# First two block sums of W2 in one group of matmuls, a new order of all steps, and 103 matmuls of constants

## The chip, the cores and the metric

The kernel runs on one core of a Trainium2 chip. Its time is the device time of one execution in microseconds, taken as the median of several runs. The engines of the core are TensorE (PE, matrix products into PSUM), VectorE (DVE), ScalarE (ACT), GpSimd (POOL) and SyncE (SP, which here only issues DMAs). Each engine works through its own queue in order; semaphores hold an instruction until what it needs is there.

## The reference

The reference is a two-way attention between tokens and a small state, followed by a feed-forward block:

```python
def _attn_ref(x, state):                      # x (8, 8, 512, 64), state (8, 8, 32, 64)
    scores = scale * np.matmul(x, state.transpose(0, 1, 3, 2))
    a = softmax(scores)
    xread = np.matmul(a, state)
    scores2 = scale * np.matmul(state, x.transpose(0, 1, 3, 2))
    a2 = softmax(scores2)
    sread = np.matmul(a2, x)
    return np.concatenate([xread, sread], axis=2)

def _moe_ref(x, g_ln, w_ch1, w_ch2):          # x (8, 544, 512), W1 (512, 2048), W2 (2048, 512)
    xn = (x - mu) / np.sqrt(var + 1e-06) * g_ln
    return x + np.maximum(xn @ w_ch1, 0.0) @ w_ch2
```

Here `softmax` stands for subtracting the row maximum, the exponential and dividing by the sum plus 1e-9, and mu and var are the mean and the variance of a row. The heads are joined between the two parts, so that a row of the second part has 512 values.

## The kernel before

All products are made in float16, with each operand split into a high and a low half and three of the four partial products kept. The feed-forward width of 2048 is cut into four *units* of 512. The work falls into these pieces, each a Python generator that yields one step after another:

- `weights1(u)`: loads one unit of W1 in two halves, packs the words, takes column means by matmuls (`means`, line 600), subtracts them, sums absolute values by matmuls with a constant matrix `ones` (`add`, line 609), scales, and splits into halves that DMAs carry to `w1c`.
- `weights2(u)`: the same kind of work for one unit of W2, which ends in `w2h[u]`.
- `attention(b)`: the attention of batch b; `state_products(b)`: the state times W1, which gives `matrix[b][u]` (line 666).
- `first_products` and `second_products_by_unit`: the feed-forward block of batch 0, unit by unit as the weights arrive (lines 702 and 716).
- `sums_of_weights(u)`: for batches 1 to 7 the second product is made by a scheme of Strassen's kind, with seven block products in place of eight. It needs sums of blocks of W2. For each unit u and each half n, four sums are made in turn: t3 = B22 - B12, then B12 - B11 (written over B12), then t2 = B22 minus the new B12, then n4 = B21 - t2. Each is four matmuls with plus or minus the identity (`signs`, line 748) into half a PSUM bank; ACT copies it out as the high half and DVE writes the low half. The first and second sum share a bank, and the third and fourth share another.
- `products(b)`: for each of two groups of columns and each unit a hidden block (`first`, line 794; for the state rows `first_of_state`, line 803) and the block products (`multiply`, line 850), then `together`, which adds the pieces up and stores.

PSUM has three pools: `ps_f` with four banks (`acc`), `ps_a` with one pair (`banks`) and `ps_d` with two banks (`half`). A tile is given a bank when a step first uses it.

The order of all steps is written out by hand in the constant `PLAN`. An entry `19:3-5` means: issue items 3 to 5 of stream 19. Streams are numbered in the order of the list `streams`: 0 the gain, 1 attention of batch 0, 2 to 5 `weights1`, 6 `state_products(0)`, 7 `first_products`, 8 to 11 `weights2`, 12 the common scale, 13 to 16 `second_products_by_unit`, 17 and 18 attention and state products of batch 1, 19 to 22 `sums_of_weights`. From 23 on each batch has eighteen streams of products (a hidden block and its block products for each of eight units and groups, in turn, with `together` at the end of each group of four) and then the attention and the state products of the next batch; so 37 and 39 are block products of batch 1, 38 the hidden block of 39, and 42 the state products of batch 2. `issue` walks the plan and issues each item, so the plan sets the order on every engine's queue. In `sums_of_weights` items 0, 3, 6 and 9 are the matmuls of the four sums for n = 0, each with its ACT copy and its DVE step behind it, and 12, 15, 18 and 21 those for n = 1. The plan need not keep items of one stream together: between 19:0 and 19:3 it may put other streams' items, and 19:1 on either side of 19:3.

The page names every step that goes through the helper `do` by line 187, and matmuls by their own lines.

Of the kernel before, what the change touches and what calls it, by code (L numbers as in the profile page):

```python
# [201 lines left out]
def moe_attention(ctx: ExitStack, tc: tile.TileContext, x, state, g_ln, w1, w2, out):  # L202
# [539 lines left out]
    def sums_of_weights(u):  # L742
# [8 lines left out]
        for n in range(2):  # L751
# [5 lines left out]
            for k, (d, a, b) in enumerate(((t3, b22, b12), (b12, b12, b11), (t2, b22, b12), (n4, b21, t2))):  # L757
                yield do(subtract, k % 2 == 0, o[k], *a, *b)
                yield do(nc.scalar.activation, d[0], o[k], AF.Copy)
                yield do(nc.vector.tensor_tensor, d[1], o[k], d[0], ALU.subtract)  # L760
# [206 lines left out]
```

## Time and profile before

| | us |
|---|---|
| median of 3 runs | 695.02 |
| lowest and highest run | 693.15, 695.36 |
| the profiled execution | 693.68 |
| its span, from first to last instruction | 691.9 |
| mean granted clock of PE | 0.977 of full |

The page gives busy times of each engine over the span; a window table gives the same for stretches of time, with the clock that PE was granted. The waits list, for each engine and line, what ended its idle time. A timeline row has the start, the time taken, the engine, the line, the operation with what it writes and reads, how many of its kind are merged in the row, and in brackets the idle time just before it with its releaser. All these rows come from the one profiled execution.

### The profile page before, as it was taken

What the parts mean: (1) busy time and instruction counts of PE and PEld (TensorE: products, weight loads), DVE (VectorE), ACT (ScalarE), POOL (GpSimd) and SP (SyncE); (2) the same over time, 40 slices, a digit from 0 to 9 for tenths busy, and PEclk for the clock granted to TensorE, in tenths of its full rate; (3) what the DMA queues carried; (4) which work ended last, traced back from release to release, by engine and by line L of the source; (5) the groups of instructions that cost most, each with busy time, mean ns of one, the idle gap of its engine ahead of it and who ended that gap; (6) DMA issues with size and microseconds to landing.
All of it is one profiled execution on the core that took longest, in us unless ns stands there. A gap on an engine that the chain in (4) does not pass through costs nothing.

```text
span 691.9 us, 14637 instructions
## 1 busy us (share of the span) xinstructions
PE 633.4 (92%) x5945; PEld 494.0 (71%) x5948; DVE 498.7 (72%) x1002; ACT 387.9 (56%) x699; POOL 215.9 (31%) x189
## 2 busy tenths in 40 slices
PE   0648897989998999999999998999999999999996
PEld 0224554546986798778877987688868877889885
DVE  4999886467666676878787777776787687646733
ACT  5498797465654565556555654475456554435332
POOL 0002242330422332533423342433444233423322
PEclk9979898999999999999999999999999999999999
DMA  8898868125340344134213330453223503144221
GB/s 326 273 253 227 245 170 163 24 39 127 95 67 17 81 124 72 38 91 139 58 47 77 95 56 20 101 135 68 64 65 110 105 1 74 39 108 77 63 63 30
DMA packets 98563, 69.63 MB, mean 101 GB/s; under 512 B 72704, under 2 KB 90624, under 8 KB 98048
## 3 DMA queue, kind: packets, MB, share of 16 engines
q1 hardware_dynamic: 96384, 64.77, 36.9%
q0 software_dynamic: 864, 3.15, 2.4%
q8 instruction: 46, 0.75, 0.5%
q10 hardware_dynamic: 1248, 0.79, 0.4%
q14 instruction: 21, 0.17, 0.1%
HBM read 28.05 MB, written 9.44 MB: 54 GB/s over the span
## 4 chain that ended last, share of the span: by engine, by line
PE 74%; DVE 14%; ACT 7%; DMA 2%; issue 2%; POOL 0%; ACTq 0%; DVEq 0%
PE acc L850 34%; PE half L794 18%; PE acc L716 5%; PE half L666 4%; PE half L803 3%; DVE rs L187 2%; PE acc L748 2%; PE acc L702 2%; PE acc L600 2%; ACT xs L187 2%; DVE w_t L187 2%; ACT sums L187 1%; DVE ts L187 1%; ACT eB L187 1%; DMA w1c<-sums 1%
## 5 line engine op out<-in xcount | busy, mean ns | idle before, releaser
L850 PEld LDWEIGHTS <-xs 128*128 128x128 f16 x2520 | 243.2, 98 | 43.3 <-issue 14.0
L187 POOL TENSOR_TENSOR xs<-rs,xs 128x512 f16<-128x512 f32 x120 | 140.3, 1181 | 270.6 <-ACT xs L187 206.9
L850 PE MATMUL acc<-w2h,xs 128*128 128x256 f16 x1440 | 184.1, 274 | 0.0
L794 PE MATMUL half<-ea,matrix 128*128 128x256 f16 x1344 | 162.7, 273 | 6.1 <-DVE matrix L187 2.7
L794 PEld LDWEIGHTS <-matrix 128*128 128x128 f16 x1344 | 130.2, 98 | 26.0 <-issue 8.0
L850 PE MATMUL acc<-sums,xs 128*128 128x256 f16 x1080 | 141.6, 273 | 0.0
L187 DVE SCALAR_TENSOR_TENSOR rs<-half,rs 128x256 f32<-128x256 f32 x224 | 89.9, 419 | 34.4 <-ACT xs L187 14.7
L187 ACT ACTIVATE xs<-half 128x256 f16<-128x256 f32 (+1 forms) x112 | 54.0, 487 | 89.3 <-DVE rs L187 39.0
L187 ACT ACTIVATE xs<-rs 128x512 f16<-128x512 f32 (+1 forms) x128 | 77.6, 619 | 41.3 <-DVE rs L187 37.5
L187 DVE SCALAR_TENSOR_TENSOR xs<-half,xs 128x256 f16<-128x256 f32 (+1 forms) x112 | 61.1, 550 | 32.4 <-ACT xs L187 30.5
L187 ACT ACTIVATE matrix<-half,hs 128x512 f16<-128x512 f32 x56 | 37.7, 684 | 30.4 <-PE half L666 30.2
L187 DVE SCALAR_TENSOR_TENSOR matrix<-half,hs,matrix 128x512 f16<-128x512 f32 x56 | 41.0, 742 | 15.3 <-ACT matrix L187 15.3
L716 PE MATMUL acc<-w2h,hid 128*128 128x512 f16 x192 | 43.1, 379 | 0.0
L187 DVE TENSOR_TENSOR strip<-acc,strip 128x256 f32<-128x256 f32 (+1 forms) x60 | 33.3, 555 | 11.8 <-PE acc L850 8.0
L187 ACT ACTIVATE rs<-half 128x256 f32<-128x256 f32 x56 | 21.3, 380 | 31.2 <-PE half L794 19.4
L666 PE MATMUL half<-w1c,sT 128*32 128x512 f16 x448 | 33.8, 384 | 2.5 <-DVE xs L187 1.2
L716 PEld LDWEIGHTS <-hid 128*128 128x128 f16 x192 | 18.5, 98 | 22.3 <-issue 1.9
L600 PE MATMUL acc<-w_t,gm 128*128 128x512 f32 x32 | 18.2, 725 | 15.7 <-DVE w_t L187 15.7
L187 POOL TENSOR_TENSOR hid<-strip,hid 128x512 f16<-128x512 f32 x16 | 19.8, 1244 | 39.5 <-ACT hid L187 39.4
L187 POOL TENSOR_TENSOR ts<-ts,mA 128x1024 f32<-128x1024 f32 (+1 forms) x8 | 15.4, 1919 | 51.5 <-DVE of_weights L187 30.1
L702 PE MATMUL acc<-ea,matrix 128*128 128x256 f16 x192 | 26.9, 301 | 2.1 <-ACT strip L187 1.1
L187 POOL TENSOR_TENSOR ts<-ts,dA 128x1024 f32<-128x1024 f32 (+1 forms) x8 | 14.4, 1806 | 45.3 <-DVE of_weights L187 23.6
(152 smaller groups left out, 783.0 us busy)
## 6 DMA issues: line engine op xcount, KB each, us to landing
raw<-in_moe_w_ch_dram SPq DMA_DIRECT2D x9, 1024.0 KB, 10.4
out_dram<-xr SPq DMA_DIRECT2D x16, 512.0 KB, 3.2
x_f<-in_x_dram SPq DMA_DIRECT2D x15, 512.0 KB, 5.6
sums<-in_moe_w_ch_dram SPq DMA_DIRECT2D x7, 1024.0 KB, 6.1
ek<-ea SPq DMA_DIRECT2D x56, 64.0 KB, 2.1
ek<-ek SPq DMA_DIRECT2D x7, 512.0 KB, 4.3
xr<-part POOLq DMA_DIRECT2D x6, 512.0 KB, 5.0
w1c<-raw SPq DMA_DIRECT2D x8, 256.0 KB, 4.2
```

The lines of the kernel that those rows point to most:

```text
L187: return lambda: f(*map(now, args), **{k: now(v) for k, v in kw.items()})
L600: nc.tensor.matmul(ps, lhsT=gm[:, k:k + 1].broadcast_to([P, P]), rhs=t4[:, k], start=k == 0, stop=k == 3)
L666: nc.tensor.matmul(ps[32 * j:32 * j + 32], lhsT=sT[:, g, a, 32 * j:32 * j + 32], rhs=w[:, 2 * g + j // 2, j % 2], start=a == 0, stop=a == ...
L702: nc.tensor.matmul(o[:, 256 * f:256 * f + 256], lhsT=m[:, g, i, P * (q + f):P * (q + f) + P], rhs=ea[:, s, k, g], start=f == 0 and g == 0 ...
L716: nc.tensor.matmul(po, lhsT=hid[:, i, q, c * P:(c + 1) * P], rhs=w[:, j, q], start=first and q == 0 and n == 0, stop=last and q == 3 and n ...
L748: nc.tensor.matmul(o, lhsT=signs[:, k // 2], rhs=v[k], start=start and k == 0, stop=k == 3, skip_group_check=True)
L794: nc.tensor.matmul(ps[:, 256 * q:256 * q + 256], lhsT=m[:, h, i, P * (2 * k + q):P * (2 * k + q) + P], rhs=ea[:, 0, j, h, 256 * g:256 * g ...
L803: nc.tensor.matmul(ps[:, 256 * q:256 * q + 256].rearrange("p (t n) -> p t n", t=2), lhsT=w[:, k // 2, k % 2, fs] if k < H else wn[:, k - H ...
L850: nc.tensor.matmul(po[o], lhsT=y[:, n, i, o] if o < 2 else x[:, o - 2, n, i], rhs=v[j], start=u == 0 and n == 0 and k == 0 and o in (2, 1, ...
```

## The change

It has three parts.

In `sums_of_weights` the matmuls of the first two sums (t3 and the new B12) become one item of eight matmuls, followed by the ACT and DVE steps of both. The third and the fourth sum stay items of four. The same matmuls run with the same operands into the same half banks. A stream of sums has 22 items now: for n = 0 the matmuls are items 0, 5 and 8, for n = 1 items 11, 16 and 19.

A new stream, 175, has 103 items. Each is one matmul of the constant `ones` (bf16, 128 x 128) with itself repeated four times (512 columns) into one tile of the pool `half` that nothing reads. They all stand in the early part of the plan: nine ahead of the first transposition of batch 0's maxima, then in groups of up to 23 between the steps of W1, the last block of eight ahead of 1:90, and three single ones behind it.

The plan is written anew for the whole kernel, with the turns that tiles take on PSUM banks accounted for. Unit 2 of W1 is treated first, then units 1, 0 and 3; before, it was 1, 0, 2 and 3. Most lines of both plans are left out here.

```diff
 PLAN = (
...
-    "7:0 1:66-67 7:1-2 7:4-5 9:0 6:9-10 9:2 7:3 7:6-7 5:12 5:9 7:12-13 5:11 7:8 5:13 17:12 17:2 17:11 5:14 6:11 8:3 "
...
-    "19:15 17:25 14:9-10 14:1 17:26-27 17:19 19:16 10:16-17 11:2 11:4 7:49 14:3 10:18-19 11:5 14:4 14:2 7:32 19:0 "
-    "7:33-34 19:17 11:6-7 19:13-14 11:8 19:1 7:35 19:3-5 20:0-1 20:3 7:44 20:2 7:45-46 17:28 17:36 17:33 15:1 17:5 "
-    "11:9 17:37 18:9 7:42 14:5 7:50 19:2 7:47 7:51 11:10-13 11:15 12:0 17:39 20:12 12:1-2 20:13-14 20:4 18:12 "
-    "20:15-16 20:5 20:17 17:4 18:10 15:3 17:3 17:6 17:34-35 15:2 7:43 17:38 17:49 15:4-5 18:11 7:52-53 7:56-58 11:14 "
...
-    "18:15 17:54 18:3 21:12 22:15 22:13 7:61 18:16 22:14 18:4 18:17 41:2 19:18 21:13-14 7:62 17:40 21:15-16 18:5 "
...
-    "18:1-2 22:17 21:6-8 18:18 22:0-1 22:3 20:21 22:2 18:19-20 20:22-23 41:3 22:4-5 23:0 23:2 23:4 23:1 23:3 21:18 "
...
+    "1:0 1:3-4 1:1-2 1:5 175:0-8 1:6-7 175:9 1:8-12 4:1 1:19 1:72 0:0 4:6 1:20 1:24-25 4:5 4:7 4:0 4:3 1:17-18 4:2 "
+    "4:4 3:1 3:6 1:22-23 1:13-14 3:5 3:7 3:0 3:3 175:10-32 4:8 3:2 1:15 3:4 175:33-36 3:8 2:0 2:3 4:9 4:12 1:21 4:11 "
+    "4:10 2:2 2:4 4:13 1:16 1:27-29 3:10 3:9 3:11 1:44 175:37-39 4:14-15 1:45-46 1:26 175:40 1:30 3:12-13 1:31 1:33 "
+    "1:47 1:34 1:48 1:35 2:1 2:6 175:41-54 3:14 2:5 4:16 5:0 5:3 17:1 5:1 2:7 3:15 1:49 3:16 1:37 1:36 1:38-39 "
+    "175:55-60 2:8 9:0 17:0 1:50 3:17 5:2 5:5 1:62 1:40 3:18-19 8:0 3:22 2:11 4:17 2:12 1:63 2:9-10 2:13 1:64 "
+    "175:61-73 1:73 1:79 1:75 1:32 2:14 3:21 1:76 5:4 4:18-19 4:21 1:80 1:51 2:15 1:58 5:6 2:16-19 2:22 17:10 5:7 "
+    "1:77-78 9:2 2:21 3:20 3:24 3:23 2:20 175:74-79 5:8 5:12 1:59-60 17:7 2:23-24 17:8 175:80-90 6:9 8:2 1:52-53 6:6 "
+    "1:74 5:11 5:10 5:9 5:13-14 6:10 1:54-55 4:20 1:56-57 6:11 5:15 6:3 6:7 1:65 17:9 6:4 5:16-18 175:91 6:0-1 6:5 "
+    "1:66-67 8:1 175:92-99 1:90 1:94 5:19 8:5 1:95 6:2 7:0 1:91-92 7:1 7:4 8:6 1:93 7:2 8:3-4 8:7 1:41 8:8 4:23 7:5 "
...
+    "5:21 175:100 8:11 7:7 8:12-13 17:14 8:15 8:14 7:13 175:101-102 17:15-18 6:13-14 1:71 7:14 1:88 1:81 8:18 6:17 "
...
+    "6:21-23 9:4-5 9:7 7:27 6:19 1:83 6:20 7:28 7:36-37 13:8 10:1 7:18 1:84-85 1:98-99 7:38 10:6 9:8 7:19 7:29 1:96 "
...
+    "10:7 10:4 10:8 13:10 10:9-10 7:50 7:35 7:31 7:41 17:29 11:2 19:11 10:11 7:51 10:12-16 10:18 10:17 10:19 17:30 "
...
+    "11:18-19 12:1 17:28 15:3 20:0 20:3 20:14 12:2 20:12-13 41:2 17:33 15:4-5 18:4-5 17:19 20:4 15:8-9 41:11 20:1-2 "
+    "20:15 15:6-7 15:10 21:11 21:14-15 17:36-37 17:39 17:38 17:40 18:7-8 21:12 7:56-58 17:4 20:16 21:16 7:59 17:3 "
...
+    "17:41-43 17:46 20:21 17:44-45 17:60-61 17:66 16:3-4 16:1-2 17:62 16:6 22:14 16:7 17:65 22:0-1 22:3 17:70 "
...
+    "22:5-6 21:5-7 17:77 25:9 27:5 25:10 17:78 22:7 21:8-9 17:79 21:10 17:80 17:85-87 25:13 22:19-21 17:88 25:11-12 "
...
+    "38:5-6 41:61 41:66 38:4 38:10 38:8 36:12 37:2 61:5 16:5 61:11 38:7 17:73 38:9 42:6-7 41:62 39:0 38:13-14 "
...
+WARM = 103
...
-            for k, (d, a, b) in enumerate(((t3, b22, b12), (b12, b12, b11), (t2, b22, b12), (n4, b21, t2))):
-                yield do(subtract, k % 2 == 0, o[k], *a, *b)
-                yield do(nc.scalar.activation, d[0], o[k], AF.Copy)
-                yield do(nc.vector.tensor_tensor, d[1], o[k], d[0], ALU.subtract)
+            for pairs in (((t3, b22, b12), (b12, b12, b11)), ((t2, b22, b12),), ((n4, b21, t2),)):
+                first = len(o)
+                def subtract_all(*v, first=first):
+                    for k in range(len(v) // 5):
+                        subtract(first != 1 and k == 0, *v[5 * k:5 * k + 5])
+                todo = [(d, a, b, o.pop(0)) for d, a, b in pairs]
+                yield do(subtract_all, *[v for d, a, b, p in todo for v in (p, *a, *b)])
+                for d, a, b, p in todo:
+                    yield do(nc.scalar.activation, d[0], p, AF.Copy)
+                    yield do(nc.vector.tensor_tensor, d[1], p, d[0], ALU.subtract)
...
+    warm = half()
+
+    def warmth():
+        for _ in range(WARM):
+            yield do(nc.tensor.matmul, warm, lhsT=ones, rhs=ones.unsqueeze(1).broadcast_to([P, 4, P]), start=True, stop=True)
+
+    streams.append(list(warmth()))
     issue(tc, streams, PLAN)
```

220 rows, old and new, of the table PLAN are left out of this document.

## The prediction

> **What bounds the kernel now.** I read the page first (busy times), then the busy table by stage, then the waits of TensorE (PE), then the timeline at the waits.
>
> ```profile
> span 691.9 us, 14637 instructions
> PE 633.4 (92%) x5945; PEld 494.0 (71%) x5948; DVE 498.7 (72%) x1002; ACT 387.9 (56%) x699; POOL 215.9 (31%) x189
> ```
>
> PE is the bound over the whole: 92% busy. What a new order can win is PE's idle time, 691.9 - 633.4 = 58.5 us, and the stretches in which its clock is below full. By stage (columns: busy us of PE, weight load, DVE, ACT, POOL, then granted clock, DMA share, GB/s):
>
> ```profile
> 20.00:80.00 60.00, 42.28 (x339) 22.84 (x341) 56.56 (x98) 46.23 (x61) 8.57 (x7) 0.85 0.93 255
> 80.00:115.00 35.00, 33.63 (x203) 18.99 (x201) 29.68 (x51) 29.37 (x43) 10.19 (x9) 0.96 0.72 175
> 115.00:166.00 51.00, 43.58 (x300) 23.48 (x300) 28.24 (x54) 28.29 (x52) 14.39 (x12) 0.93 0.32 70
> 166.00:450.00 284.00, 277.08 (x2809) 229.10 (x2806) 212.08 (x443) 157.74 (x309) 98.83 (x83) 0.99 0.32 74
> 450.00:686.00 236.00, 233.95 (x2298) 198.10 (x2295) 159.11 (x333) 116.17 (x220) 83.19 (x72) 1.00 0.30 71
> 686.00:691.90 5.90, 0.00 (x0) 0.00 (x0) 2.02 (x3) 0.00 (x0) 0.00 (x0) 0.87 0.33 89
> ```
>
> PE's idle time is 17.7 us from 20 to 80, 1.4 to 115, 7.4 to 166, 6.9 to 450 and 2.1 to 686. The tail after 686 has 5.9, and the first 20 us have the rest, 58.5 - 35.5 - 5.9 = 17.1. From 20 to 80 DVE is busy 56.56 of 60 us: there the bound is VectorE, which builds the weights, and idle PE costs little. From 115 to 166 neither DVE (28.24 of 51) nor ACT (28.29) is full, and yet PE stands still for 7.4 us. Who holds it there:
>
> ```profile
> PE acc L600 <- DVE w_t L187: 15.7, 2, 8.6
> PE acc L748 <- ACT sums L187: 4.4, 3, 3.4
> PE acc L748 <- DVE sums L187: 4.0, 2, 2.4
> ```
>
> L748 is the group of matmuls that forms one block sum of W2. It waits five times, 8.4 us in all. The five places, and one eviction at each kind:
>
> ```profile
> 113.46 0.60 PE L748 MATMUL acc<-w2h,signs 128*128 128x256 f16 x4
> 115.16 1.91 ACT L187 ACTIVATE sums<-w_t 128x2048 bf16<-128x2048 f32 x1
> 117.07 0.36 ACT L187 ACTIVATE sums<-acc 128x256 f16<-128x256 f32 x1
> 117.48 1.87 PE L748 MATMUL acc<-w2h,signs 128*128 128x256 f16 x8 [3.42 <-ACT sums L187]
> 119.82 1.01 PE L748 MATMUL acc<-w2h,signs 128*128 128x256 f16 x4 [0.47 <-ACT sums L187]
> 120.62 2.77 PE L702 MATMUL acc<-ea,matrix 128*128 128x256 f16 x12
> 130.91 0.60 PE L748 MATMUL acc<-w2h,signs 128*128 128x256 f16 x4 [1.58 <-DVE sums L187]
> 148.84 0.42 DVE L187 TENSOR_TENSOR sums<-acc,sums 128x256 f16<-128x256 f32 x1
> 149.32 0.60 PE L748 MATMUL acc<-w2h,signs 128*128 128x256 f16 x4 [2.41 <-DVE sums L187]
> 165.11 0.81 PE L748 MATMUL acc<-w2h,signs 128*128 128x256 f16 x6 [0.47 <-ACT sums L187]
> ```
>
> The first sum of unit 0 ends at 114.06. ACT first does the long pass of 1.91 us over the last W2 unit, then evicts that sum at 117.07 to 117.43, and 0.05 us later PE starts the second. These need no data from one another: they lie in the two halves of one PSUM bank. In the plan of before, stream 19 has its reader 19:1 ahead of the second group 19:3. Likewise 20:1 is ahead of 20:3, 20:13-14 ahead of 20:15, 21:13-14 ahead of 21:15 and 22:1 ahead of 22:3. These are the five waits, no more and no less; the three other pairs have no reader in between, and no wait.
>
> **The change part by part.** *One group for two sums.* The eight matmuls of the first two sums are one plan item, so no reader can stand between them. No matmul is added or dropped; the evictions are as many as before. Removed: 8.4 us of waits on an engine that is the bound. What is late next: the third sum needs the second's evictions, but at least 32 matmuls stand between them in the new plan (21:11 to 21:16), against two pairs of evictions of 0.36 and 0.42 us. The fourth needs the third's; its least cover is 28 matmuls (21:5 to 21:8), for one such pair. **-8.4.** Ends: 0, if another wait takes each place, and -8.4.
>
> *The clock behind these waits.* Rows with the same work at full and at reduced clock, and the clock itself:
>
> ```profile
> 77.30:85.00 7.70, 7.70 (x55) 5.03 (x53) 6.21 (x15) 4.63 (x8) 1.77 (x2) 0.64 0.93 239
> 115.00:125.00 10.00, 7.05 (x37) 3.95 (x37) 1.73 (x5) 4.68 (x9) 2.13 (x3) 0.66 0.42 86
> 106.08 1.05 PE L748 MATMUL acc<-w2h,signs 128*128 128x256 f16 x8
> 142.17 1.47 PE L702 MATMUL acc<-ea,matrix 128*128 128x256 f16 x12
> 77.31 6.78 PE L702 MATMUL acc<-ea,matrix 128*128 128x256 f16 x36
> ```
>
> After the 3.42 us wait the clock is 0.66, and L748 x8 takes 1.87 instead of 1.05, x4 1.01 instead of 0.60, L702 x12 2.77 instead of 1.47: 0.8 + 0.4 + 1.3 = 2.5 us. Without the wait PE has no gap there: **-2.5** (ends 0 and -2.5).
>
> *103 matmuls of constants.* Each is 128x512 in bf16, as L609 is (the second row is from the groups by line: busy, mean ns of one):
>
> ```profile
> 28.20 1.02 PE L609 MATMUL acc<-raw,ones 128*128 128x512 bf16 x4 [0.83 <-ACT raw L187]
> ...
> L609 PE MATMUL acc<-raw,ones 128*128 128x512 bf16 x10 | 3.0, 378 | 2.0 <-ACT raw L187 1.9
> ...
> 18.03 8.79 PE L600 MATMUL acc<-w_t,gm 128*128 128x512 f32 x16 [7.12 <-DVE w_t L187]
> 41.27 5.68 PE L600 MATMUL acc<-w_t,gm 128*128 128x512 f32 x8 [8.61 <-DVE w_t L187]
> 55.54 3.70 PE L600 MATMUL acc<-w_t,gm 128*128 128x512 f32 x8
> DVE w_t L187 <- PE acc L600: 2.6, 3, 1.1
> ```
>
> The column means of W1 cost 8.79 for two units and 5.68 for one where PE had stood still, and 3.70 where it had not: 1.4 and 2.0 us slower. DVE, the bound there, waited for them 2.6 us in all. If they run at full clock, most of that goes: **-1.9** (ends 0 and -2.6). The same holds for the products of batch 0 at 77.31, where 36 matmuls took 6.78. At full clock L702 x12 takes 1.47 and L748 x8, of the same width, 1.05, so a matmul takes 0.42 / 4 = 0.105 and 36 take 1.47 + 24 x 0.105 = 4.0: 2.8 us lost. The new plan has its last block of eight constants before these products and only three after it, so I take half: **-1.4** (ends 0 and -2.8).
>
> Their cost: L609 x4 has (1.02 - 0.38) / 3 = 0.21 us between starts, so 103 need 22 us at full clock and 44 at half. PE's idle time up to 80 us is 17.1 + 17.7 = 34.8 us. At full clock they fit; at half they overrun by 9 us. They wait for nothing but a constant, but PE takes its matmuls in the order of the plan, and behind them are queued the means and sums of W1 (blocks of 23, 14, 6, 13 and 11), for which DVE and ACT wait. I take **0**, as the blocks are there to hold the clock up, and keep +9 as an end.
>
> A rule of the Trainium skill bears on these clock terms: "TensorE: Matmul & The Clock Gate", part 1, says that the gate opens after about 3.4 us of sustained activity, and that the ramp costs under 1% of a typical kernel. This case differs in the first point: from 77.3 to 85.0 PE is busy without a break at a clock of 0.64, which is 5.5 us at half speed. By the page each of the three gaps would cost 1.7 us at most, and the sum below would change by less than 1 us.
>
> *The order anew.* The early steps stand otherwise: W1's unit 2 is now the first to be treated, and the first products of batch 0 (7:0) come behind nine more DVE instructions: three w_t steps, a row maximum, a matrix, an ea and three scalars. By these rows that is 2.06 + 0.68 + 0.68 + 0.69 + 3 x 0.15 = 4.6 us.
>
> ```profile
> 62.20 0.69 DVE L187 SCALAR_TENSOR_TENSOR ea<-ef,ea 128x512 f16<-128x512 f32 x1
> 62.81 2.06 DVE L187 SCALAR_TENSOR_TENSOR w_t<-w_t,gx,acc 128x512 f32<-128x512 f32 x3
> 65.04 0.68 DVE L187 SCALAR_TENSOR_TENSOR matrix<-acc,matrix 128x512 f16<-128x512 f32 x1
> 69.76 0.68 DVE L187 TENSOR_REDUCE of_weights<-acc 128x1 f32<-128x512 f32 x1
> 70.47 0.15 DVE L187 TENSOR_SCALAR of_weights<-of_weights 128x1 f32<-128x1 f32 x1
> ```
>
> It is caught up: ahead of the item 13:8, a second product of batch 0, stand 127 DVE instructions in place of 133. **0**, with +4.6 as an end. Queues: five loads of W1 still go to SP ahead of its first transposes, as before; no queue is passed that was not.
>
> *Steady state.* After 166 us and ahead of the tail PE idles 6.9 + 2.1 = 9.0 us, half of it for these:
>
> ```profile
> PE half L794 <- DVE matrix L187: 2.7, 3, 2.0
> PE half L794 <- DVE xs L187: 2.1, 2, 1.8
> ```
>
> The order of some 500 PE items is new there. Nothing in the trace shows it; it may lose all of these waits (-9.0) or have twice as many (+9.0). Read off the plan, it cuts both ways. Between a hidden block and its first products the old plan has 26, 26, 34 and 38 matmuls at its four closest places; the new one has 20 (38:5 to 39:0), then 42, 44 and 48. But the new plan takes a hidden bank again with no PE item between its last reader and the next writer 31 times, the old one 11 times, and that is where the L794 waits on xs lie. I take **+2.0**.
>
> Sum: -8.4 - 2.5 - 1.9 - 1.4 + 2.0 = -12.2 us; span 691.9 - 12.2 = 679.7. The profiled execution took 693.68, 1.8 more than its span, and the median of the runs shown is 695.02, another 1.3 more: **682.8, say 683 us**, 1.7% faster.
>
> **The rivals.**
> 1. *PE starts too late (slower).* The first products of batch 0 stood at 59.7 us, and up to 77.3 PE did the work of this row:
>
> ```profile
> 59.70:77.30 17.60, 13.61 (x153) 9.77 (x150) 17.43 (x29) 16.59 (x24) 5.32 (x4) 0.96 0.88 260
> ```
>
> If the constants and the later first products push all of it, 13.6 us, behind 77 us and the clock falls once more (2.8), 16.4 us come back: span 679.7 + 16.4 = 696.1, time 699. It decides once more than 12.2 us are pushed. For it: 4.6 us more DVE work ahead of 7:0, 103 matmuls in order. Against: DVE, not PE, sets the pace to 80 us.
> 2. *The waits move.* The 7.4 us from 115 to 166 reappear at the next step (the fourth sums, the last W2 unit), and the change saves only the early terms, -1.9 - 1.4 + 2.0: span 690.6, time 694. Against: DVE and ACT are little over half busy there.
> 3. *The steady state is mended too.* Half of its 9.0 us goes, instead of +2.0: span 673, time 676. For it: nothing in the trace, only that the whole order is new.
>
> **How the numbers follow.** Forecast 0.53, rival 1 0.14, rival 2 0.13, rival 3 0.20. The forecast's own range is 677 to 690: its terms without the two early ones and with steady waits of +6, or with steady waits of -4. The range for 8 in 10: its low end has every term at its best (-8.4 - 2.5 - 2.6 - 2.8 - 9.0 = -25.3, about 670, with a chance of a few in a hundred, so 671); its high end takes in rival 2 and the lower half of rival 1: 697. About 0.3% (2 us) is what a measurement of this kernel can tell from no change. Faster by more: forecast, rival 3 and a quarter of rival 2, 0.76. Within: most of rival 2, 0.10. Slower: 0.14.
>
> **What would show it.** Right, if L748 has no wait of over 1 us on ACT or DVE, the clock from 115 to 125 is 1.0, the means take about 3.7 us per unit, DVE waits under 1 us for L600, and PE's idle time from 115 to 166 falls under 2 us. Wrong, if PE's useful work up to 88 us is clearly less than before (rival 1), if another line takes over L748's waits (rival 2), or if the idle time after 166 us is far from 11 us.

## The result and the profile after

The changed kernel takes **667.13 us** (median of 4 runs, 666.29 to 667.89) against 694.85 us before (4 runs on the same chip, 693.15 to 695.36): a ratio of 0.9605, 95% interval 0.9585 to 0.9625. That is 27.7 us less, where the prediction had 12 less. The direction was right, the time lies below the range, and the sum was less than half of what happened.

The head of the page of the changed kernel, then its busy table by stage, with the columns of the table before (busy us of PE, weight load, DVE, ACT, POOL, then granted clock, DMA share, GB/s):

```profile
span 665.1 us, 14886 instructions
PE 643.9 (97%) x6051; PEld 499.6 (75%) x6051; DVE 499.5 (75%) x1002; ACT 388.8 (58%) x699; POOL 217.9 (33%) x189
```

```profile
0.00:20.00 20.00, 15.26 (x46) 5.98 (x47) 12.86 (x30) 10.34 (x16) 0.70 (x6) 0.91 0.92 325
20.00:80.00 60.00, 51.17 (x428) 27.57 (x430) 56.74 (x97) 47.57 (x64) 7.31 (x6) 1.00 0.98 253
80.00:115.00 35.00, 34.99 (x226) 20.06 (x219) 26.43 (x48) 31.83 (x47) 13.99 (x13) 1.00 0.59 151
115.00:166.00 51.00, 51.00 (x447) 33.37 (x445) 38.81 (x83) 35.28 (x71) 13.54 (x11) 1.00 0.54 111
166.00:450.00 284.00, 283.04 (x2867) 234.74 (x2865) 221.91 (x455) 162.19 (x317) 107.14 (x88) 1.00 0.31 75
450.00:660.00 210.00, 208.40 (x2050) 177.83 (x2048) 141.26 (x291) 101.63 (x189) 75.23 (x65) 1.00 0.29 72
660.00:665.10 5.10, 0.00 (x0) 0.00 (x0) 1.46 (x3) 0.00 (x0) 0.00 (x0) 0.87 0.38 103
```

Set each stage's idle time of PE beside that of before. From 80 to 115 us it falls from 1.4 us to 0, and from 115 to 166 from 7.4 to 0. For the rest, count up to PE's last matmul, which ends at 685.88 us before and at 659.32 here (so 0.7 of the 1.6 us that PE idles in the row from 450 to 660 belong to the tail): after 166 us PE's idle time falls from 8.9 to 1.9, and the tail, from 6.0 to 5.8, hardly changes. These are 16.0 of the 26.8 us by which the span is shorter. The granted clock is 1.00 in every stage after 20 us in which PE works. The first two rows can't be compared as busy time, because 103 matmuls of constants are counted in them. The longest waits of PE, over the whole span (engine, tile and line; who releases it; us in total, times, longest):

```profile
PE acc L667 <- DMA w1c<-raw: 3.5, 1, 3.5
PE banks L188 <- DVE x_am L188: 3.0, 1, 3.0
PE acc L610 <- ACT raw L188: 1.7, 2, 1.3
PE half L188 <- DVE ones L309: 1.1, 1, 1.1
PE half L667 <- DVE rs L188: 1.0, 1, 1.0
PE half L667 <- DVE xs L188: 0.9, 1, 0.9
```

The five waits of the block sums are gone (their line is now L749, and no row names it), and so are those of the hidden blocks (now L801). Line numbers differ by kernel: a hidden block's group is L793 to L795 in kernels without the group of two sums and L799 to L801 in those with it, the state products are L665 to L667, and the helper is L186 to L188.

### The profile page after: what moved, and what is told of

Same layout as the page of the kernel before. It is cut to its first block, busy times and chain, and to the rows that moved or that the text cites. A ratio compares the mean times of both kernels' runs of the same rounds, so it can differ in the third digit from the quotient of the medians.

```text
span 665.1 us, 14886 instructions
## 1 busy us (share of the span) xinstructions
PE 643.9 (97%) x6051; PEld 499.6 (75%) x6051; DVE 499.5 (75%) x1002; ACT 388.8 (58%) x699; POOL 217.9 (33%) x189
## 4 chain that ended last, share of the span: by engine, by line
PE 86%; DVE 8%; DMA 3%; ACT 1%; issue 1%; SPq 0%; DVEq 0%
PE acc L857 41%; PE half L801 22%; PE acc L717 6%; PE half L667 5%; PE half L810 3%; DVE w_t L188 2%; PE acc L703 2%; PE acc L749 2%; PE banks L481 1%; PE banks L405 1%; PE banks L517 1%; DMA w1c<-raw 1%; DMA raw<-in_moe_w_ch_dram 1%; PE banks L494 1%; DMA x_f<-in_x_dram 1%
## 5 line engine op out<-in xcount | busy, mean ns | idle before, releaser
L188 POOL TENSOR_TENSOR xs<-rs,xs 128x512 f16<-128x512 f32 x120 | 142.5, 1200 | 272.6 <-ACT xs L188 207.1
L801 PE MATMUL half<-ea,matrix 128*128 128x256 f16 x1344 | 159.4, 273 | 0.0
L801 PEld LDWEIGHTS <-matrix 128*128 128x128 f16 x1344 | 130.7, 98 | 16.7 <-issue 0.8
L188 DVE SCALAR_TENSOR_TENSOR rs<-half,rs 128x256 f32<-128x256 f32 x224 | 89.4, 419 | 27.6 <-ACT rs L188 13.3
L188 ACT ACTIVATE xs<-rs 128x512 f16<-128x512 f32 x128 | 77.1, 618 | 40.5 <-DVE rs L188 33.8
L188 ACT ACTIVATE xs<-half 128x256 f16<-128x256 f32 (+1 forms) x112 | 53.7, 487 | 73.2 <-PE half L801 51.3
L188 DVE SCALAR_TENSOR_TENSOR xs<-half,xs 128x256 f16<-128x256 f32 (+1 forms) x112 | 61.2, 550 | 28.1 <-ACT xs L188 24.5
L188 ACT ACTIVATE matrix<-half,hs 128x512 f16<-128x512 f32 x56 | 38.1, 687 | 35.2 <-PE half L667 34.9
L188 DVE SCALAR_TENSOR_TENSOR matrix<-half,hs,matrix 128x512 f16<-128x512 f32 x56 | 41.2, 742 | 16.0 <-ACT matrix L188 15.3
L188 ACT ACTIVATE rs<-half 128x256 f32<-128x256 f32 x56 | 21.4, 382 | 42.4 <-PE half L801 40.0
L188 DVE TENSOR_TENSOR strip<-acc,strip 128x256 f32<-128x256 f32 (+1 forms) x60 | 33.2, 554 | 10.5 <-PE acc L857 7.5
L667 PE MATMUL half<-w1c,sT 128*32 128x512 f16 x448 | 33.5, 384 | 1.9 <-DVE rs L188 1.0
L188 POOL TENSOR_TENSOR ts<-ts,mA 128x1024 f32<-128x1024 f32 (+1 forms) x8 | 14.4, 1806 | 59.3 <-DVE mA L188 52.9
L188 PE MATMUL half<-ones 128*128 128x512 bf16 x103 | 28.0, 416 | 1.1 <-DVE ones L309 1.1
L188 DVE SCALAR_TENSOR_TENSOR x<-x_f,x_s,x 128x512 f16<-128x512 f32 x32 | 24.8, 799 | 5.3 <-ACT x L188 5.3
L188 POOL TENSOR_TENSOR hid<-strip,hid 128x512 f16<-128x512 f32 x16 | 19.5, 1232 | 26.9 <-ACT hid L188 26.8
L188 DVE BATCH_NORM_STATS2 s<-xr 128x6 f32<-128x512 f32 x32 | 21.6, 684 | 8.7 <-ACT xr L188 8.6
```

The lines of the kernel that those rows point to most:

```text
L188: return lambda: f(*map(now, args), **{k: now(v) for k, v in kw.items()})
L667: nc.tensor.matmul(ps[32 * j:32 * j + 32], lhsT=sT[:, g, a, 32 * j:32 * j + 32], rhs=w[:, 2 * g + j // 2, j % 2], start=a == 0, stop=a == ...
L801: nc.tensor.matmul(ps[:, 256 * q:256 * q + 256], lhsT=m[:, h, i, P * (2 * k + q):P * (2 * k + q) + P], rhs=ea[:, 0, j, h, 256 * g:256 * g ...
```

## The experiments

Two theories stood at the outset. **A**: the group of two sums and the late part of the order remove PE waits that nothing hides. **B**, its rival for each part: a gain there is taken up by something else, by the loads and VectorE early, by the next wait late. The medians below are always beside runs of before on the same chip.

### The constants left out

```
-    streams.append(list(warmth()))
-    ... 175:0-8 ... 175:10-32 ... 175:100-102 ...   (out of the plan)
```

> The changed kernel without its 103 matmuls of constants; everything else in its order. Theory A (the clock sets part of the early stage): the means of W1 (L601) go back from 3.7 us per unit to between 4 and 5.7, the granted clock in the first 60 us falls below 0.9, VectorE waits again 2 to 3 us for L601, and the time rises by 2 to 5 us, to 669 to 672 us. Theory B (VectorE's own work sets the early stage, the clock is hidden): the clock falls all the same, the time stays within 1 us of 667.1.

Measured: 667.71 us, ratio 0.9614 (0.9594 to 0.9633), the time of the changed kernel within what can be told apart. The means of W1 and the first state products in this run:

```profile
16.19 9.50 PE L599 MATMUL acc<-w_t,gm 128*128 128x512 f32 x16 [6.70 <-DVE w_t L186]
35.12 5.06 PE L599 MATMUL acc<-w_t,gm 128*128 128x512 f32 x8
58.00 1.90 PE L665 MATMUL acc<-w1c,sT 128*32 128x512 f16 x16 [3.68 <-DMA w1c<-raw]
76.38 4.10 PE L701 MATMUL acc<-ea,matrix 128*128 128x256 f16 x36
```

The same in the changed kernel:

```profile
16.16 3.70 PE L601 MATMUL acc<-w_t,gm 128*128 128x512 f32 x8 [0.48 <-DVE w_t L188]
57.91 1.05 PE L667 MATMUL acc<-w1c,sT 128*32 128x512 f16 x16 [3.50 <-DMA w1c<-raw]
66.38 4.10 PE L703 MATMUL acc<-ea,matrix 128*128 128x256 f16 x36
```

Without constants the means do run slowly: 9.50 us for two units, 5.06 for one. But both kernels then stand before the same transfer, which brings the narrow W1 at 57.9 or 58.0 us, and whatever was won before it is lost in that wait. Behind the wait the kernel without constants is slower again for a moment (1.90 against 1.05 us in these rows, and 2.74 against 1.48 for its first twelve products), and at 87 us the same matmuls stand 1.0 us later in its profile. So the constants do hold the clock up, but the medians differ by only 0.6 us and their intervals overlap: a gain of about 1 us is neither shown nor excluded. The last row of the first fence matters as well: 36 first products in 4.10 us, at full clock and without one constant.

### The constants alone, in the order of before

```
+    streams.append(list(warmth()))
     ...  9 constants ahead of 1:6, 23 ahead of 3:8, 36 ahead of 4:8, 5 each ahead of 8:9, 8:11, 17:15  ...
```

> Before's program and plan with the 103 constant matmuls added, the blocks put ahead of the same kinds of items as in the changed kernel (most ahead of the column means of W1 and of the attention of batch 0). Theory A (the prediction's clock terms): the means run at full clock, DVE waits less for them and the first products of batch 0 run faster; the time falls by 2 to 4 us, to 690 to 692. Theory B (the gain is swallowed by the loads and by VectorE, which set the pace up to 76 us): the granted clock from 20 to 80 us rises above 0.95, the means fall to about 3.7 us for eight, and the time stays within 1.5 us of before.

Measured: 693.03 us (10 runs, 690.05 to 698.88) against 694.31, ratio 0.9985 (0.9958 to 1.0012): no difference that can be told, though a gain of up to 2.9 us isn't excluded. The products of batch 0, whose 36 took 6.78 us at 77.31 before:

```profile
77.00 1.25 PE L188 MATMUL half<-ones 128*128 128x512 bf16 x5
78.64 4.10 PE L703 MATMUL acc<-ea,matrix 128*128 128x256 f16 x36
```

They run at full clock now, but start 1.33 us later, behind 15 constants, and end at 82.74 in place of 84.09. That is a lead of 1.35 us, the size of the prediction's 1.4, and these two profiled executions keep it to the end (spans of 690.5 and 691.9 us). But it can't be put down to the constants: the state products behind these 36 start at 82.67 us here and at 84.02 before, and in four other runs with the same early order and no constants at 82.71, 84.98, 85.04 and 85.91. One execution differs from the next by more than the lead.

### The group alone, in the order of before

```
-  19:0 ... 19:1 ... 19:3 ... 19:4      (first sum, its reader, second sum, its reader)
+  19:0 ... 19:1 ... 19:3               (both sums in 19:0, then the readers; so for all eight pairs)
```

> The kernel before with nothing changed but the first two block sums made by one group of eight matmuls, which stands in the plan where the first sum stood. Theory A (the five waits are a fault of their own): TensorE waits no more at these matmuls, idle time from 115 to 166 us falls from 7.4 us to under 2, the clock from 115 to 125 returns to 1.0, and the time falls by 8 to 11 us, to 684 to 687 us. Theory B (the waits move to the next step, such as the later sums or the last unit of W2): the idle time comes back at other lines, and the time falls by 0 to 4 us, to 691 to 695 us.

Measured: 681.69 us against 694.17, ratio 0.9816 (0.9795 to 0.9838): 12.5 us, more than the 10.9 that the prediction had for waits and clock. The stage, and two places further on:

```profile
115.00:166.00 51.00, 51.00 (x423) 32.00 (x422) 36.84 (x77) 35.87 (x73) 16.01 (x14) 1.00 0.46 105
```

```profile
208.41 1.47 PE L800 MATMUL half<-ea,matrix 128*128 128x256 f16 x12 [2.02 <-DVE matrix L187]
209.72 1.47 PE L856 MATMUL acc<-w2h,xs 128*128 128x256 f16 x12
```

Before, the same place read:

```profile
218.79 2.20 PE L794 MATMUL half<-ea,matrix 128*128 128x256 f16 x12 [2.02 <-DVE matrix L187]
220.78 2.46 PE L850 MATMUL acc<-w2h,xs 128*128 128x256 f16 x12
```

PE is busy 51.00 of 51.00 us at full clock, so no other wait took the place of the five. And the wait of 2.02 us on the matrix is still there, to the digit, but the 24 matmuls behind it take 2.94 us in place of 4.66. These 1.7 us are as large as the surplus; why this wait lowered the clock in one kernel and not in the other was not settled. The group is not what spares it: in two more runs with the late order of before, one without the group (the constants alone) and one with it (the early order alone, below), the same wait of 2.02 us is followed by 4.66 us for these 24 matmuls.

### The late order alone

```
   before's plan up to the last item of the block sums (19 to 22)
+  from there on every item in the order of the changed kernel
```

> The kernel before, its plan up to the last item of the block sums, then all that is left in the order of the changed plan; no constants, no grouping. Theory A (late order has a gain of its own): idle time after the sums under 4 us and the time 685 to 689 us. Theory B (it has none): 693 to 696 us.

Measured: 684.75 us against 694.17, ratio 0.9857 (0.9833 to 0.9881): 9.4 us less. The waits of the block sums stay (4.4 and 4.0 us in all). PE's waits from 166 us on:

```profile
PE half L665 <- DVE rs L186: 1.0, 1, 1.0
PE half L665 <- DVE xs L186: 0.9, 1, 0.9
PE banks L515 <- ACT xr L186: 0.8, 1, 0.8
```

No hidden block waits any more (a fourth wait, of 0.5 us, is the last one of the block sums). Here the prediction had +2.0 us.

### The early order alone, with the group and the constants

```
   the changed kernel's plan up to the last item of the block sums
-  from there on the order of the changed kernel
+  from there on the order of before
```

> The changed kernel's plan up to the last item of the block sums, then all that is left in the order of the plan before. Theory A (the late order has a gain of its own): the waits of L801 on VectorE and of the state products come back, idle time of TensorE between 166 us and the tail is 7 to 11 us, and the time is 673 to 677 us. Theory B (these waits were a consequence of the late start, and vanish with it): the idle time stays under 4 us and the time within 2 us of 667.1.

Measured: 680.67 us against 694.17, ratio 0.9803 (0.9781 to 0.9825), so 13.5 us slower than the changed kernel, and slower than either theory expected. The late waits are all back (2.02 us on the matrix again, now at 206.81), and the seam, where the two plans are joined, adds 1.90 us at 175.91; PE idles 8.9 us from 166 to 450. A wait of 1.5 us on a transfer (sT) stands in this profile and not in that of the changed kernel. Because of the seam this run gives the size of the late order less cleanly than the run before it.

### Group and late order, without the early order and the constants

```
   before's plan with the group up to the last block sum, then the changed kernel's order; no constants
```

> The group of two sums, before's order up to the last block sum and the changed kernel's order from there, no constants. Theory A (group and late order are separate gains of 12.8 and 9.9 us): 694 - 12.8 - 9.9 = 671, range 669 to 674; what is left to the changed kernel's 667, some 4 us, belongs to the early order. Theory B (both take the same idle time, or the late order needs the early one): 676 or more.

Measured: 672.70 us against 694.31, ratio 0.9687 (0.9670 to 0.9703). That is 21.6 us, and the two parts alone gave 12.5 + 9.4 = 21.9: they add up. To the changed kernel without constants (667.71) 5.0 us are left for the early order, with a wait of 0.8 us at the seam of this run (on ACT xr) in them. One row is still as before:

```profile
78.12 6.93 PE L702 MATMUL acc<-ea,matrix 128*128 128x256 f16 x36
```

Against the 4.10 us above these are 2.8 us. In the 6 us ahead of these 36 products PE is busy for 4.14 us here and 4.14 before, and for 4.96 in the run without constants, where the clock holds; that the busier stretch is the reason fits these rows but was not tested by itself. Nor is this row the net gain, since other early matmuls are slow in the run without constants (the means above): over the whole span its PE is busy 1.2 us less than here (626.7 against 627.9) and idle 3.5 us less (39.4 against 42.9), 0.8 of them at the seam.

### The group undone in the new order

```
-  19:0 (both sums)  ...  19:3  19:4  ...  19:1  19:2
+  19:0 (first sum)  ...  19:1  19:2  ...  19:3 (second sum)  19:4 ...      (so for all eight pairs)
```

> The changed kernel with the constants and its order, but each first pair of block sums is two plan items again: the first sum stands where the group stood, then its evictions, and the second sum stands behind them. Theory A (a second sum behind the first one's readers waits for their evictions, whatever the order around it): at least four waits of TensorE at the line of the sums between 80 and 166 us, together 4 us or more, a reduced clock behind the longest of them, time 673 to 682. Theory B (the new order alone covers the evictions): no wait over 1 us there, time within 3 us of the changed kernel, 667 to 670.

Measured: 671.74 us (668.57 to 672.24), ratio 0.9662 (0.9632 to 0.9692), 4.6 us more than with the group. PE's waits from 76 us on:

```profile
PE acc L749 <- ACT sums L188: 2.3, 4, 0.7
PE half L667 <- DMA sT<-sh: 1.6, 1, 1.6
...
PE acc L749 <- DVE sums L188: 0.3, 1, 0.3
```

Neither theory is right as it stood. Five waits return at the line of the sums, but they are 2.6 us in all and none reaches 0.8 us; the clock stays at 1.00. The new order has more room around the evictions: before, the longest of these waits (3.42 us) stood behind ACT's pass of 1.91 us over a W2 unit. So group and early order overlap: the group is worth 12.5 us in the old order and about 4 in the new one (671.74 against 667.13 and 667.64, the two medians of the changed kernel). That is more than the 2.6 us of waits. Part of the rest can be estimated from the rows of sums: four matmuls alone take 0.60 us and eight 1.04, so one more costs 0.11, and of the 0.60 about 0.16 us are the end of the last matmul, which the next one normally covers and which lies bare ahead of each wait, five times 0.16 = 0.8 us. The wait of 1.6 us on a transfer is no part of it, since the changed kernel shows it too in another run (1.5 us, below).

### What the late waits are: three moves on VectorE

Before's chain at the longest of them, on DVE and PE:

```profile
216.85 1.25 DVE L187 STREAM_TRANSPOSE ts<-banks 128x1024 f32<-128x1024 f32 x1 [2.88 <-ACT eB L187]
218.03 0.71 DVE L187 SCALAR_TENSOR_TENSOR matrix<-half,hs,matrix 128x512 f16<-128x512 f32 x1
```

DVE stands idle for 2.88 us at a transpose of the attention scores, until ACT has done two exponentials. Behind it in DVE's queue is the second half of the matrix, whose inputs were there since 214.79, and PE waits for that matrix. The second longest, at 430.90, begins with this:

```profile
426.25 1.92 POOL L187 TENSOR_TENSOR ts<-ts,mA 128x1024 f32<-128x1024 f32 x1 [4.37 <-DVE mA L187]
426.42 1.77 DVE L187 TENSOR_SCALAR rB<-sumB 128x2 f32<-128x2 f32 x1
428.10 1.33 DVE L187 SCALAR_TENSOR_TENSOR rs<-half,rs 128x256 f32<-128x256 f32 x3
429.52 0.60 ACT L187 ACTIVATE xs<-half 128x512 f16<-128x512 f32 x1 [3.70 <-DVE rs L187]
```

A scalar of 128x2 takes 1.77 us, three reads of hidden banks stand behind it, and ACT, which reads the next, waits 3.70 us.

```
-  41:38 42:5                      (transpose of the scores, second half of the matrix)
+  42:5 41:38
-  96:8 101:46 96:3 96:7 96:9      (101:46 is the scalar, the rest reads of hidden banks)
+  96:8 96:3 96:7 96:9 101:46
-  81:44-45 82:12 ... 82:13-14     (attention step and its transfer, second half of a matrix)
+  82:12 ... 82:13-14 81:44-45
```

> Before's program and plan with three VectorE items moved by a few places, nothing else: the second half of the matrix ahead of the transpose of the attention scores (at 218 us), one 128x2 scalar of the attention behind three reads of hidden banks (at 426 us), and one attention step behind the second half of a matrix (at 361 us). TensorE's own order is untouched. Theory A (the steady waits are single places where VectorE takes an attention step ahead of the read that TensorE waits for): the waits of 2.02, 1.80 and 0.47 us go, and with the first the 1.8 us that its reduced clock cost; time lower by 4 to 7 us, 687 to 690. Theory B (VectorE and ScalarE are at their limit there, so that the waits move to the next block): within 2 us of before.

Measured: 689.15 us against 694.31, ratio 0.9926 (0.9908 to 0.9945): 5.2 us from three moves, with PE's order as it was. The first place now:

```profile
213.48 0.75 DVE L187 SCALAR_TENSOR_TENSOR matrix<-half,hs,matrix 128x512 f16<-128x512 f32 x1 [0.85 <-ACT matrix L187]
215.27 1.47 PE L794 MATMUL half<-ea,matrix 128*128 128x256 f16 x12
215.52 1.25 DVE L187 STREAM_TRANSPOSE ts<-banks 128x1024 f32<-128x1024 f32 x1 [1.29 <-ACT eB L187]
```

The matrix is done before the transpose, and PE starts without a wait. The three waits that were aimed at, 4.3 us in all, are gone, though about 1.5 us came back in small waits elsewhere: those of the state products (L666) grow from 2.3 to 3.6 us in all. So these late waits come from single places in VectorE's queue; had VectorE been short of time there, all of them should have come back.

### The same for what is left in the changed kernel

Its two late waits (0.96 us at 273.96, 0.92 us at 472.81) stand behind these, the first also behind the attention step that follows (1.92 us at 270.96):

```profile
268.70 1.91 POOL L188 TENSOR_TENSOR ts<-ts,mA 128x1024 f32<-128x1024 f32 x1 [3.97 <-DVE mA L188]
268.93 1.71 DVE L188 TENSOR_SCALAR rB<-sumB 128x2 f32<-128x2 f32 x1
469.84 1.92 POOL L188 TENSOR_TENSOR ts<-ts,mA 128x1024 f32<-128x1024 f32 x1 [2.15 <-DVE mA L188]
470.13 2.18 DVE L188 SCALAR_TENSOR_TENSOR sk<-s_r,x_s,sk 64x512 f16<-64x512 f32 x1
```

```
-  61:46 ... 56:8 ... 61:47 ... 61:44-45 ... 56:10 ... 56:9
+  56:8 ... 56:10 ... 56:9 61:46-47 61:44-45     (scalars and attention step behind the reads)
-  121:35 ... 116:4
+  116:4 121:35                                  (product of the state behind one read)
```

> The changed kernel with five VectorE instructions and one transfer that hangs on them moved by a few places, TensorE's order untouched: at 269 us the 128x2 scalar, its reciprocal and scaling and one attention step behind three reads of hidden banks, at 470 us one 64x512 product of the state behind one such read. Theory A (the changed kernel's two last steady waits, 0.96 and 0.92 us, come from VectorE instructions that are stretched from 0.16 to 1.71 us and from 0.75 to 2.18 us beside a GpSimd instruction and stand ahead of the read that TensorE waits for): both waits go, TensorE idles under 1 us between 166 and 660 us, time lower by 1 to 2 us, 665 to 666. Theory B (the next read is late as well): both waits stay or come back one block on, time as the changed kernel, 667.

> The changed kernel once more on the same chip, to stand beside the run with the two moves: 666 to 668.

Measured: 665.90 us with the moves (4 runs, 664.42 to 667.60, ratio 0.9595, 0.9573 to 0.9617), 667.64 us without (5 runs, 665.82 to 668.49, ratio 0.9615, 0.9594 to 0.9636). The longest waits of PE after 76 us, first with the moves, then without:

```profile
PE half L667 <- DMA sT<-sh: 0.6, 1, 0.6
PE acc L703 <- DVE matrix L188: 0.3, 1, 0.3
PE half L801 <- DVE xs L188: 0.3, 1, 0.3
```

```profile
PE half L667 <- DMA sT<-sh: 1.5, 1, 1.5
PE half L667 <- DVE rs L188: 1.0, 1, 1.0
PE half L667 <- DVE xs L188: 0.9, 1, 0.9
```

Both waits are gone from the trace, and the median is 1.7 us lower, as expected; but the intervals overlap, so the time alone doesn't prove a version faster than the changed kernel. These rows also show that the wait on the transfer sT varies from run to run of one kernel (1.5 us here, none in the profile of the changed kernel above).

## Why the prediction was off, step by step

| step | forecast | measured |
|---|---|---|
| group of two sums, with the clock behind | -8.4 - 2.5 | -12.5 (alone, in the old order) |
| order in the steady state | +2.0 | -9.4 (alone) |
| early order | 0 | -5.0 (672.70 to 667.71) |
| constants | -1.9 - 1.4 | -0.6, within the uncertainty |
| sum | -12.2 | -27.5 (whole change: -27.7) |

The last column is less of a test than it looks. The early order and the constants are differences between one kernel and the next on the way to the changed one, so they fill whatever group and late order leave; only that those two add up (21.9 and 21.6) is a finding.

**The group: mechanism right, size nearly.** The five waits were where the plan had the first sum's reader ahead of the second group; joined, they went, and no other took their place. That rules out rival 2. The term was 1.6 us short. The clock loss behind the matrix wait at 218.79 (1.7 us), which was not in the sum, went too in the run with the group alone, but not in the other run that kept the late order and had the group, so that share may be luck.

**The steady state: the step that failed.** The prediction judged the late order by two counts of PE items, the matmuls between a hidden block and its first products and the number of times a bank is taken again at once, and took +2.0 us between -9.0 and +9.0. Neither count sees what the waits hang on. The releasing engine was named in the rows that were quoted (DVE matrix, DVE xs, DVE rs); the question was what stands ahead of that instruction in DVE's queue. The chain at 218.79 answers it, and three moves there gave 5.2 us. Rival 3 had the sign, at half the size (4.5 us less waiting) and with a chance of 0.20; in the changed kernel PE's idle time from 166 us to its last matmul fell from 8.9 to 1.9, and the clock loss behind the matrix wait (1.7) went with it: 8.7 us. The waits on state products, 2.3 us before and 1.9 after, were moved by no run in the old order; in the changed kernel two moves on VectorE took them away. The prediction's own mark for this, idle time after 166 us far from 11 us, is the one that struck.

**The early order: 0 was wrong, and so was the sign of its end.** The first products did come later, 63.94 in place of 59.72: 4.2 us for the 4.6 worked out from DVE's rows. But that is not a cost when PE waits there anyway. The clock of the products is one thing that counted: 36 stand at 66.38 and take 4.10 us, where before 36 stood at 77.31 and took 6.78. Less idle time of PE is the larger share of what the early order won (above); which of its moves brought it was not tried. Rival 1 looked at the same step and priced only the delay.

**The constants: right in the rows, wrong in the time.** Means at 3.70 us per unit, DVE waiting under 1 us for them, 36 products at full clock: each mark that was set for them was met. But the gain of the means ends at the transfer of W1 at 58 us, and that of the 36 products needs no constants in the new order. The second step that failed is taking a faster PE as a gain in a stretch of which the prediction itself said that PE isn't the bound. The cost of the constants, 0, was right.

**The range.** Its low end had every term at its best, 670, and was cut to 671 as a rare case. The terms that were missing (1.7 us of clock and the early order's gain) lie below it, and -9.0 for the steady state was treated as an extreme, although the three waits that were tried, about half of that time, had one kind of cause.

## What to carry to other kernels

When an engine that is the bound waits for another, follow the releaser's own queue backwards: the instruction ahead of it that waits for something else, or that is many times longer than its like, is the fault, and moving one item can mend it. A clock or a stretch that runs faster is worth time only up to the next wait that both versions meet; find that wait (here a transfer at 58 us) before counting the gain. Parts that relieve the same place overlap: a part's worth is known only together with the order in which it was tried (12.5 us for the group in the old order, about 4 in the new one). And before a difference of 1 us between two profiles is given a cause, look at the same row in other runs of the same stretch: here it moved by over 3 us with nothing changed ahead of it.

## What the hardware showed that was not expected

**A small VectorE instruction can take ten times its time beside a GpSimd instruction.** The scalar step on 128x2 takes 0.16 us in five of its eight places before, as here, without GpSimd:

```profile
231.59 0.16 DVE L187 TENSOR_SCALAR rB<-sumB 128x2 f32<-128x2 f32 x1
```

In the other three a GpSimd instruction runs beside it, and it takes 1.12, 1.14 and 1.77 us. In the rows above it takes 1.77 us and ends at 428.19, GpSimd's at 428.17; in the changed kernel it takes 1.71 and ends at 270.64, GpSimd's at 270.61. The product of the state, 0.75 us where GpSimd doesn't run, takes 2.18 and ends 0.55 us after GpSimd's. Not every small step suffers: the reciprocal on the same 128x2 takes 0.15 to 0.17 us in all eight places before, also at 436.35 in the midst of a GpSimd instruction. Reads of PSUM aren't stretched, as the run with three moves shows, where four of them stand beside the same GpSimd instruction at 0.42 us each:

```profile
422.29 1.66 DVE L187 SCALAR_TENSOR_TENSOR rs<-half,rs 128x256 f32<-128x256 f32 x4
422.45 1.91 POOL L187 TENSOR_TENSOR ts<-ts,mA 128x1024 f32<-128x1024 f32 x1 [4.37 <-DVE mA L187]
```

The Trainium skill, "SBUF — State Buffer", section "SBUF: two separate sides", says that the two engines share a pair of ports as an exclusive lock, taken by GpSimd, or by a VectorE instruction in a fast mode or with two SBUF inputs (the latter only against a GpSimd instruction that reads SBUF), for the whole instruction. The trace agrees: the scalar ends within 0.03 us of GpSimd's instruction, and reads of PSUM are let through. No row shows whether the scalar ran in a fast mode.

**A wait of the same length costs the clock in some runs and not in another.** Behind 2.02 us on the matrix 24 matmuls took 4.66 us before, with the constants alone and with the early order alone, and 2.94 with the group alone. The Trainium skill, "TensorE: Matmul & The Clock Gate", part 1, says that the clock is set by a free-running window of activity of some 3.4 us; by that, two equal waits could end differently, depending on where in the window they fall. No run here varied only the moment of the wait, so this stays open.
